# Retention and a squared-ReLU feed-forward on one core: first casts on VectorE, fillers from one zero tile, joined retention clusters from a later group

## The chip, the cores and the metric

The kernel runs on one core of a Trainium2 chip. Its time is the device time of the whole program in microseconds (us), the median of several executions. A profile is taken of one execution; its span runs from the first to the last instruction. Engines are named as in the profile: PE (TensorE; PEld is its weight loads), DVE (VectorE), ACT (ScalarE), POOL (GpSimd) and SP (SyncE, whose queue issues nearly all DMAs here).

## The reference

```python
scores = scale * np.matmul(q, k.transpose(0, 1, 3, 2))     # 8 batches, 8 heads, 576 positions, 64 per head
gamma = 1.0 - 2.0 ** (-5.0 - np.arange(H))
Dmat = np.where(rel >= 0, gamma[:, None, None] ** rel[None, :, :], 0.0)   # rel = i - j
x = np.matmul(scores * Dmat[None], v)                      # causal, decaying with distance
x = x.transpose(0, 2, 1, 3).reshape(4608, 512)
h = x @ w_in                                               # 512 -> 2048
out = (np.maximum(h, 0) ** 2) @ w_out                      # 2048 -> 512
```

All inputs and the output are float32.

## The kernel before

**Units and groups.** The 4608 rows are cut into 36 units of 128: four per batch ("full"), and for every two batches one more that holds the last 64 positions of both ("tail"). Groups are one unit, one unit, and then 17 times two units. A group g goes through retention, which gives its `xT`, and through the feed-forward.

**Retention of a group.** Keys and queries are needed transposed (`kqT`). Then PE makes the scores (`psc`) and the state sums (`psS`, keys times values), DVE masks the scores (`rT`) and carries the states on (`Rm`, `stmp`, `R`), PE makes the outputs (`psO`, from states and from masked scores), and DVE scales these into `xT`. All of these products are 64x64, on quarters of the array. In an unjoined group this is two clusters on PE: `fa` (scores and sums), and `fb` (outputs, with a drain of PE between its two halves). From group `JOIN` on (line 218), clusters are joined: `f1` holds the first outputs of g and the scores of g+1, `f2` the sums of g+1 and the other outputs of g, and there is no drain. `add_casts` gives the casts of groups behind `JOIN` a due time one group earlier.

**Feed-forward of a group.** `ph` = x times w_in (64 matmuls of 256 columns, line 730), ACT's ReLU into `rl`, a square into `gT`, then times w_out into `po`: plainly for the first three groups and the last (line 771), and by seven Strassen products of half size for the others (line 823; DVE makes the sums `gS`).

**The start.** SP issues the first loads in the order of `FIRST`: the first pair of units (k, q, v; `p0`), a quarter of w_in, another, the second pair (`p2`), the other two quarters of w_in, the four quarters of w_out. They share four staging buffers ("wst"), so that a load can wait for the casts of an earlier one. Each weight quarter is cast to float16 half by POOL and half by ACT (line 306). The first four units come in as pairs (`add_unit_pair`): each row of a load is two neighbouring positions. k, q and v are cast as they are (`kx`, `qx`, `vx`, lines 395 and 398; k and v on POOL, q on ACT), PE transposes `kx` and `qx` (line 411) and brings rows of `kx` and `vx` into order by products with the permutation `perm` (`psn`, line 432). From unit 8 on, the transposes are DMA transposes on SP (line 363).

**Fillers.** 40 matmuls of 128x512 into one PSUM tile (`warm`, line 234) have the lowest priority and take the PE time for which the planner has nothing else. They read `ident` as weights and the zero tile `junk`, which DVE sets after its other constants (line 211).

**The planner.** Every step is a task with an engine, a due key, a duration and dependencies (`Schedule`). It plays the program through once with these durations, takes on each engine the ready task with the lowest key, and emits the instructions in the order that results. So durations decide an order that the hardware then follows: each engine runs its queue in order[...]. The planned durations of loads (`dma_task`), transposes (line 364) and stores (lines 783 and 877) are such numbers.

Of the kernel before, what the change touches and what calls it, by code (L numbers as in the profile page):

```python
# [10 lines left out]
FP16 = mybir.dt.float16  # L11
# [90 lines left out]
def kernel(  # L102
# [54 lines left out]
    w_out16 = const.tile([P, NF, DM], FP16, name="w_out16")  # L157


    ident = const.tile([P, P], FP16, name="ident")  # L160
    make_identity(nc, ident)

# [44 lines left out]
           "tail": gam_f[:, :, 0:64].rearrange("p n (c i) -> p c n i", c=1).to_broadcast([P, 2, NP, 64])}  # L207
    dec128 = const.tile([P, NP], FP32, name="dec128")
    nc.scalar.activation(out=dec128, in_=lnrow_R, func=ACTF.Exp, scale=128.0)
    junk = const.tile([P, 512], FP16, name="junk")  # L210
    nc.vector.memset(junk, 0.0)


    L = 2 * NF
    WARM = 40
    EARLY = 20
    SQ_ACT = (0, 1, 2, 3, 4, 5, 6)
    JOIN = 9
    XBAR = 8
    PAIRED = 4  # L220
    FIRST = ["p0", "w0", "w1", "p2", "w2", "w3", "w4", "w5", "w6", "w7"]
# [9 lines left out]
    def warm():  # L231
        if not warm_ps:
            warm_ps.append(ps_ff.tile([P, 512], FP32, name="warm", tag="ff"))
        nc.tensor.matmul(warm_ps[0], lhsT=ident, rhs=junk, start=True, stop=True)
    fill = []
    for _ in range(WARM):
        fill.append(add("PE", 10 ** 6, 0.3, warm, deps=fill[-1:], acq=() if fill else ("ff",)))
    sched.free("ff", fill[-1:])


# [14 lines left out]
    def dma_task(key, dur, fn, **kw):  # L255
        t = add("SP", key, dur, fn, deps=list(last_load), **kw)
        last_load[:] = [t]
        return t
# [18 lines left out]
    def add_load_pair(u):  # L277
        b, c = units[u][1:]
        for n, (name, src) in enumerate((("k", k), ("q", q), ("v", v))):
            def fn(n=n, name=name, src=src):  # L280
                if name != "q":
                    tile_of["stage", u] = stage.tile([P, 2, H, 2 * D], FP32, name="pair", tag="wst")
                x = tile_of[name + "32", u] = tile_of["stage", u][:, n % 2]
                nc.sync.dma_start(out=x, in_=src[b, :, c * P:(c + 2) * P, :].rearrange("h (p e) d -> p h (e d)", e=2))  # L284
            loaded[name, u] = loaded[name, u + 1] = dma_task(0, 1.4 if loaded else 2.3, fn,
                                                             acq=("wst",) if name != "q" else ())

    def add_weight(i):
# [41 lines left out]
    def add_unit(u, base):  # L330

        kind, b, c = units[u]
        tail = [tail_dec] if kind == "tail" else []
        xbar = u >= XBAR

        def sorted_cast(op, out_, in_):
            op(out=out_.rearrange("p (n b a d) -> p n b a d", n=2, b=2, a=2),  # L337
               in_=in_.rearrange("p (n a b) d -> p n b a d", n=2, a=2))

        def fk():  # L340
            t = tile_of["kq", u] = cast.tile([P, 2, H * D], FP16, name="kq16", tag="kq16")
            sorted_cast(nc.gpsimd.tensor_copy, t[:, 0], tile_of["k32", u])

        def fq():
            sorted_cast(nc.gpsimd.tensor_copy, tile_of["kq", u][:, 1], tile_of["q32", u])

        def fv():
            t = tile_of["v16", u] = cast.tile([P, H, D], FP16, name="v16", tag="v16")
            nc.gpsimd.tensor_tensor(  # L349
                out=t, in0=tile_of["v32", u],  # L350
                in1=vdec[kind].rearrange("p (h o) -> p h o", o=1).to_broadcast([P, H, D]), op=ALU.mult)
        ck = add("POOL", base, 0.65, fk, deps=[loaded["k", u]], acq=("kq",))
        cq = add("POOL", base + 1, 0.62, fq, deps=[loaded["q", u], ck])
        cv = add("POOL", base + 2, 1.1, fv, deps=[loaded["v", u]] + tail, acq=("v16",))
        for what, t in (("k", ck), ("v", cv)):
            for w in gate.get((what, u), []):
                sched.need(w, t)
        T["casts", u] = [ck, cq, cv]
        sched.free("ld", [ck, cq, cv])
        if xbar:  # L360
            def fx2():
                t = tile_of["kqT", u] = work.tile([P, 2 * NP, P], FP16, name="kqT", tag="kqT", bufs=6)
                nc.sync.dma_start_transpose(out=t, in_=tile_of["kq", u].rearrange("p x n -> p (x n)"))  # L363
            T["kqT", u] = [add("SP", -1, 2.0, fx2, deps=[ck, cq], acq=("kqT",), after=4.0)]
            return
        T["kqT", u] = []
        for i, cst in enumerate((ck, cq)):
            def ft(i=i):
                tile_of["psT", u, i] = ps_ff.tile([P, NP, P], FP16, name="psT", tag="ff")
                for hp in range(NP):  # L370
                    nc.tensor.transpose(tile_of["psT", u, i][:, hp, :], tile_of["kq", u][:, i, hp * P:(hp + 1) * P],
                                        ident)

            def fe(i=i):
                if i == 0:
                    tile_of["kqT", u] = work.tile([P, 2 * NP, P], FP16, name="kqT", tag="kqT", bufs=6)
                (nc.vector.tensor_copy if i else nc.scalar.copy)(
                    out=tile_of["kqT", u][:, i * NP:(i + 1) * NP], in_=tile_of["psT", u, i])
            t = add("PE", base + L + i, 0.22, ft, deps=[cst], acq=("ff",))
            e = add("DVE" if i else "ACT", base + L + 2 + i, 0.42 if i else 0.59, fe, deps=[t] + T["kqT", u],  # L380
                    acq=() if i else ("kqT",))
            sched.free("ff", [e])
            T["kqT", u].append(e)


    def add_unit_pair(u, base):

        xs = {}
        for name, eng, op in (("k", "POOL", nc.gpsimd.tensor_copy), ("q", "ACT", nc.scalar.copy),
                              ("v", "POOL", nc.gpsimd.tensor_copy)):  # L390
            def fc(name=name, op=op):
                t = tile_of[name + "x", u] = cast.tile([P, 2, H * D], FP16, name=name + "x", tag="kq16")
                x = tile_of[name + "32", u].rearrange("p h (e d) -> p h e d", e=2)
                if name == "v":
                    op(out=t.rearrange("p e (h d) -> p e h d", d=D), in_=x.rearrange("p h e d -> p e h d"))
                    return
                for e in range(2):
                    op(out=t[:, e].rearrange("p (n b a d) -> p n b a d", n=2, b=2, a=2),
                       in_=x[:, :, e].rearrange("p (n a b) d -> p n b a d", n=2, a=2))
            xs[name] = add(eng, base + "kqv".index(name), dict(k=1.3, q=1.2, v=1.2)[name], fc, deps=[loaded[name, u]],  # L400
                           acq=("kq",))
        sched.free("wst", [xs["k"], xs["q"]])
        sched.free("wst", [xs["v"]])
# [312 lines left out]
    def add_ff(g):  # L716
# [44 lines left out]
        for s, u in enumerate(us):  # L761
            end = base2 + NF * (s + 1)
            f2 = T["ff2"][-1:] if s == 0 else f2[-1:]

            cuts = [(0, DM)] if u != groups[-1][-1] else [(0, HM), (HM, DM)]
            for ci, (lo, hi) in enumerate(cuts):
                for fi in range(NF):
                    def f(fi=fi, s=s, u=u, lo=lo, hi=hi):
                        if fi == 0:
                            tile_of["po", u, lo] = ps_ff.tile([P, hi - lo], FP32, name="po", tag="ff")  # L770
                        nc.tensor.matmul(tile_of["po", u, lo], lhsT=tile_of["g", g][:, fi, s * P:(s + 1) * P],  # L771
                                         rhs=w_out16[:, fi, lo:hi], start=(fi == 0), stop=(fi == NF - 1))
                    f2.append(add("PE", base2 + NF * s + fi / len(cuts) + 8 * ci, 0.0025 + 0.2135 / len(cuts), f,
                                  deps=[sq[fi // nf]] + wcast[4 + fi // 4] + f2[-1:],
                                  acq=("ff",) if fi == 0 else ()))

                def fo(u=u, lo=lo, hi=hi):
                    if lo == 0:
                        tile_of["o", u] = o_pool.tile([P, DM], FP32, name="o", tag="o")
                    nc.scalar.copy(out=tile_of["o", u][:, lo:hi], in_=tile_of["po", u, lo])  # L780
                oc = add("ACT", end + 1, 0.12 + 0.47 / len(cuts), fo, deps=[f2[-1]], acq=() if lo else ("o",))
                sched.free("ff", [oc])
                st = add(*(("ACT", end + 1.1, 0.05) if g == len(groups) - 1 else ("SP", -0.5, 0.6)),
                         lambda u=u, lo=lo, hi=hi: store(u, tile_of["o", u], lo, hi), deps=[oc], after=2.5)
            sched.free("o", [st])
        sched.free("g", [f2[-1]])
# [2 lines left out]
    def add_strassen(g, us, base, sq):  # L789
# [84 lines left out]
        sched.free("g", [p4])  # L874
        T["ff2"].append(p4)
        for u, ds in ((uA, [d11, c12]), (uB, [d22, d21])):
            st = add("SP", -0.5, 0.6, lambda u=u: store(u, o_tile(u)), deps=ds, after=2.5)
            sched.free("o", [st])

    for g in range(len(groups)):  # L880
# [44 lines left out]
```

## Time and profile before

| | |
|---|---|
| median of 6 executions | 300.6 us (298.77 to 304.06) |
| the profiled execution | 298.77 us, span 296.8 us |
| granted TensorE clock | 1.00 |
| PE busy | 285.9 us (96%), 4464 matmuls |
| DVE, ACT, POOL busy | 192.0, 189.5, 97.1 us |
| moved by DMA | 54.16 MB, 145503 packets, 130481 of them under 512 B |
| chain that ended last, by engine | PE 77%, DMA 13%, SP's queue 5% |

A busy share is an average over stages. The page's part 2 cuts the span into 40 slices of 7.4 us; a digit of 9 stands for a slice that is at least 90% busy, and PEclk is the granted clock. A DMA share is the mean over 16 engines. Matmul records overlap, since matmuls are pipelined: the time from one start to the next tells more than a record's length. Lines such as L730 are lines of the kernel before; in the changed kernel everything behind line 212 stands one line earlier.

### The profile page before, as it was taken

The numbers are of one execution on the slowest core, as the hardware profiler recorded it, in microseconds if no ns is written. First come the engines' busy times: TensorE is split into PE (matmuls) and PEld (weight loads), VectorE is DVE, ScalarE is ACT, GpSimd is POOL, SyncE is SP. The second block draws the span as 40 slices with busy tenths as digits, with TensorE's granted clock in tenths as the row PEclk, the third lists the DMA queues.
The fourth block names the chain that finished last, engine by engine and source line by source line (L and its number), as shares of the span: only waits on it lengthen the run. The fifth ranks groups of instructions, "written<-read, shape, count | busy, mean of one in ns | idle before, by whom it ended". The sixth has DMA issues, their size and how long they took to land.

```text
span 296.8 us, 10350 instructions
## 1 busy us (share of the span) xinstructions
PE 285.9 (96%) x4464; PEld 235.2 (79%) x4464; DVE 192.0 (65%) x409; ACT 189.5 (64%) x355; POOL 97.1 (33%) x130
## 2 busy tenths in 40 slices
PE   4997899999999999999999999999999999999995
PEld 1456667588888888888888888888888888888874
DVE  1287579678477877587876767668777766462410
ACT  4556554286767757575758575857585768558861
POOL 5454486444242432524244343517251100000000
PEclk9999999999999999999999999999999999999999
DMA  8999979899799998989999999999999420101012
GB/s 207 360 336 385 336 164 251 173 227 179 180 198 214 210 157 207 195 196 188 234 151 241 181 202 182 195 231 215 233 164 215 124 73 2 73 3 73 0 73 71
DMA packets 145503, 54.16 MB, mean 182 GB/s; under 512 B 130481, under 2 KB 136881, under 8 KB 145457
## 3 DMA queue, kind: packets, MB, share of 16 engines
q1 hardware_dynamic: 145008, 52.97, 86.2%
q8 instruction: 35, 0.57, 0.8%
q10 hardware_dynamic: 448, 0.52, 0.7%
q14 instruction: 12, 0.09, 0.1%
HBM read 36.70 MB, written 9.44 MB: 155 GB/s over the span
## 4 chain that ended last, share of the span: by engine, by line
PE 77%; DMA 13%; SPq 5%; issue 1%; POOL 1%; ACT 1%; POOLq 0%
PE ph L730 36%; PE po L823 27%; PE po L771 7%; DMA wi<-in_moe_w_in_dram 7%; DMA q<-in_q_dram 5%; PE psO L324 4%; SPq L270 2%; PE psc L324 1%; PE psS L324 1%; DMA kqT<-kq 1%; SPq L363 1%; SPq L284 1%; POOL w_in L306 1%; SPq L294 1%; POOL kq L337 1%
## 5 line engine op out<-in xcount | busy, mean ns | idle before, releaser
L730 PE MATMUL ph<-xT,w_in 128*128 128x256 f16 (+1 forms) x1216 | 139.5, 267 | 2.3 <-issue 2.1
L730 PEld LDWEIGHTS <-w_in 128*128 128x128 f16 x1216 | 112.6, 98 | 16.8 <-issue 2.5
L738 ACT ACTIVATE rl<-ph 128x512 f16<-128x512 f32 x144 | 84.7, 588 | 49.9 <-PE ph L730 46.5
L748 ACT ACTIVATE gT<-rl 128x512 f16<-128x512 f16 x112 | 70.5, 630 | 3.6
L801 DVE TENSOR_TENSOR gS<-gT 128x512 f16<-128x512 f16 x60 | 29.8, 497 | 41.1 <-ACT gT L748 40.4
L823 PEld LDWEIGHTS <-gS 128*128 128x128 f16 x480 | 45.8, 98 | 6.2 <-DVE gS L801 0.5
L823 PE MATMUL po<-wT,gS 128*128 128x256 f16 x360 | 49.0, 273 | 0.0
L349 POOL TENSOR_TENSOR v<-v,vdec_full 128x512 f16<-128x512 f32 x28 | 30.4, 1087 | 38.1 <-DMA v<-in_v_dram 29.2
L823 PEld LDWEIGHTS <-gT 128*128 128x128 f16 x360 | 35.0, 98 | 4.1
L337 POOL CAST kq<-k 128x512 f16<-128x512 f32 x32 | 22.3, 698 | 35.4 <-DMA k<-in_k_dram 34.5
L337 POOL CAST kq<-q 128x512 f16<-128x512 f32 x32 | 21.6, 674 | 34.8 <-DMA q<-in_q_dram 34.8
L823 PE MATMUL po<-w_out,gT 128*128 128x256 f16 x240 | 31.1, 273 | 0.0
L616 DVE TENSOR_TENSOR xT<-psO,gam_full 128x512 f16<-128x512 f32 x36 | 23.9, 685 | 7.6 <-PE psO L324 7.5
L555 DVE TENSOR_TENSOR rT<-psc,mask 128x512 f16<-128x512 f32 x36 | 24.1, 682 | 4.0 <-PE psc L324 4.0
L750 DVE TENSOR_TENSOR gT<-rl 128x512 f16<-128x512 f16 x32 | 17.7, 555 | 13.0 <-ACT rl L738 12.8
L771 PE MATMUL po<-w_out,gT 128*128 128x512 f16 (+1 forms) x112 | 23.2, 349 | 0.0
L846 DVE TENSOR_TENSOR o<-po,u 128x256 f32<-128x256 f32 x30 | 12.6, 420 | 8.5 <-ACT u L836 6.0
L836 ACT COPY u<-po 128x256 f32<-128x256 f32 x30 | 11.0, 366 | 10.2 <-PE po L823 10.1
L801 DVE TENSOR_TENSOR gS<-gT,gS 128x512 f16<-128x512 f16 x30 | 16.0, 533 | 1.0
L801 DVE TENSOR_TENSOR gS<-gS,gT 128x512 f16<-128x512 f16 x30 | 15.5, 517 | 1.0
L771 PEld LDWEIGHTS <-gT 128*128 128x128 f16 x112 | 10.4, 98 | 7.0
L584 DVE TENSOR_TENSOR R<-stmp,dec 128x256 f16<-128x256 f32 x28 | 15.1, 538 | 0.9
(75 smaller groups left out, 254.3 us busy)
## 6 DMA issues: line engine op xcount, KB each, us to landing
out_dram<-o SPq DMA_DIRECT2D x31, 256.0 KB, 3.0
k<-in_k_dram SPq DMA_DIRECT2D x28, 256.0 KB, 4.8
q<-in_q_dram SPq DMA_DIRECT2D x28, 256.0 KB, 5.0
v<-in_v_dram SPq DMA_DIRECT2D x28, 256.0 KB, 5.0
wi<-in_moe_w_in_dram SPq DMA_DIRECT2D x4, 1024.0 KB, 8.6
wo<-in_moe_w_out_dram SPq DMA_DIRECT2D x4, 1024.0 KB, 10.5
pair<-in_k_dram SPq DMA_DIRECT2D x2, 512.0 KB, 5.1
pair<-in_q_dram SPq DMA_DIRECT2D x2, 512.0 KB, 6.4
```

The lines of the kernel that those rows point to most:

```text
L324: nc.tensor.matmul(out_, lhsT=lhsT, rhs=rhs, start=start, stop=True, skip_group_check=True, tile_position=(64 * row, 64 * col))
L337: op(out=out_.rearrange("p (n b a d) -> p n b a d", n=2, b=2, a=2), in_=in_.rearrange("p (n a b) d -> p n b a d", n=2, a=2))
L349: nc.gpsimd.tensor_tensor(out=t, in0=tile_of["v32", u], in1=vdec[kind].rearrange("p (h o) -> p h o", o=1).to_broadcast([P, H, D]), op=ALU. ...
L555: nc.vector.tensor_tensor(out=r, in0=tile_of["psc", g][:, :, cols(s)].rearrange("p a (n i) -> p a n i", i=64), in1=mask.rearrange("p (o r ...
L616: nc.vector.tensor_tensor(out=tile_of["x", g][:, :, s * P:(s + 1) * P].rearrange("p n (c i) -> p c n i", c=2), in0=tile_of["psO", g][:, :, ...
L730: nc.tensor.matmul(tile_of["ph", g, fb][:, j, :], lhsT=w_in16[:, m, fi * P:(fi + 1) * P], rhs=tile_of["x", g][:, m, :], start=(m == 0), st ...
L738: nc.scalar.activation(out=t, in_=tile_of["ph", g, fb], func=ACTF.Relu)
L748: nc.scalar.activation(out=t, in_=rl, func=ACTF.Square)
L750: nc.vector.tensor_tensor(out=t, in0=rl, in1=rl, op=ALU.mult)
L771: nc.tensor.matmul(tile_of["po", u, lo], lhsT=tile_of["g", g][:, fi, s * P:(s + 1) * P], rhs=w_out16[:, fi, lo:hi], start=(fi == 0), stop= ...
L801: nc.vector.tensor_tensor(out=Sx(k, h), in0=in0(h), in1=in1(h), op=op)
L823: nc.tensor.matmul(tile_of["pb", g, bank], lhsT=left(i), rhs=right[:, i, :], start=(start and i == 0), stop=(i == HF - 1), skip_group_chec ...
```

## The change

Five edits in one:

- `junk` is set as DVE's first instruction, and the fillers take a slice of it as weights instead of `ident`. Their planned durations become 0.43 for the first eight and 0.216 for the others.
- The casts of the first pair (u = 0) go to DVE; those of the second pair stay with POOL, ACT, POOL.
- `JOIN` goes from 9 to 12, so that groups 9, 10 and 11 keep unjoined clusters, and casts get the earlier due time from group 13 on instead of 10.
- The planned durations of the paired loads, of the DMA transposes and of the stores change.
- The planned durations of the paired casts go by engine.

```diff
+    junk = const.tile([P, 512], FP16, name="junk")
+    nc.vector.memset(junk, 0.0)
     ident = const.tile([P, P], FP16, name="ident")
     make_identity(nc, ident)
...
     nc.scalar.activation(out=dec128, in_=lnrow_R, func=ACTF.Exp, scale=128.0)
-    junk = const.tile([P, 512], FP16, name="junk")
-    nc.vector.memset(junk, 0.0)
...
-    JOIN = 9
+    JOIN = 12
...
-        nc.tensor.matmul(warm_ps[0], lhsT=ident, rhs=junk, start=True, stop=True)
+        nc.tensor.matmul(warm_ps[0], lhsT=junk[:, 0:P], rhs=junk, start=True, stop=True)
     fill = []
-    for _ in range(WARM):
-        fill.append(add("PE", 10 ** 6, 0.3, warm, deps=fill[-1:], acq=() if fill else ("ff",)))
+    for i in range(WARM):
+        fill.append(add("PE", 10 ** 6, 0.43 if i < 8 else 0.216, warm, deps=fill[-1:], acq=() if fill else ("ff",)))
...
-            loaded[name, u] = loaded[name, u + 1] = dma_task(0, 1.4 if loaded else 2.3, fn,
+            loaded[name, u] = loaded[name, u + 1] = dma_task(0, 1.6 if loaded else 3.0, fn,
                                                              acq=("wst",) if name != "q" else ())
...
-            T["kqT", u] = [add("SP", -1, 2.0, fx2, deps=[ck, cq], acq=("kqT",), after=4.0)]
+            T["kqT", u] = [add("SP", -1, 2.7, fx2, deps=[ck, cq], acq=("kqT",), after=3.0)]
...
-        for name, eng, op in (("k", "POOL", nc.gpsimd.tensor_copy), ("q", "ACT", nc.scalar.copy),
-                              ("v", "POOL", nc.gpsimd.tensor_copy)):
+        pool, act, dve = (("POOL", nc.gpsimd.tensor_copy), ("ACT", nc.scalar.copy), ("DVE", nc.vector.tensor_copy))
+        for name, (eng, op) in (("k", pool if u else dve), ("q", act if u else dve), ("v", pool if u else dve)):
...
-            xs[name] = add(eng, base + "kqv".index(name), dict(k=1.3, q=1.2, v=1.2)[name], fc, deps=[loaded[name, u]],
+            xs[name] = add(eng, base + "kqv".index(name), dict(POOL=1.2, ACT=1.15, DVE=0.85)[eng], fc, deps=[loaded[name, u]],
...
-                st = add(*(("ACT", end + 1.1, 0.05) if g == len(groups) - 1 else ("SP", -0.5, 0.6)),
+                st = add(*(("ACT", end + 1.1, 0.05) if g == len(groups) - 1 else ("SP", -0.5, 0.7)),
...
-            st = add("SP", -0.5, 0.6, lambda u=u: store(u, o_tile(u)), deps=ds, after=2.5)
+            st = add("SP", -0.5, 0.7, lambda u=u: store(u, o_tile(u)), deps=ds, after=2.5)
```

## The prediction

> **What bounds the kernel now.** First the page's part 2, to see which stages there are.
>
> ```profile
> PE   4997899999999999999999999999999999999995
> ...
> PEclk9999999999999999999999999999999999999999
> DMA  8999979899799998989999999999999420101012
> ```
>
> PE is full from the sixth slice (37 us) to the end, and its clock is granted in full throughout. Only the first five slices are open, and in these the DMA row is full. The stretch view (length; busy time and instructions of PE, weight loads, DVE, ACT, POOL; clock; DMA share; GB/s) says it more sharply:
>
> ```profile
> 2.30:13.00 10.70, 8.65 (x44) 4.02 (x44) 1.01 (x18) 4.66 (x12) 4.46 (x11) 1.00 1.09 336
> 13.00:19.00 6.00, 5.86 (x104) 2.68 (x105) 4.56 (x8) 3.33 (x5) 2.76 (x4) 1.00 1.19 301
> 19.00:35.00 16.00, 13.73 (x343) 10.85 (x328) 12.06 (x23) 10.38 (x16) 7.87 (x9) 1.00 1.05 382
> 35.00:42.00 7.00, 6.76 (x57) 4.88 (x56) 3.73 (x7) 5.08 (x8) 4.53 (x6) 1.00 0.93 193
> 60.00:130.00 70.00, 69.52 (x1156) 60.37 (x1154) 49.69 (x101) 48.85 (x93) 26.93 (x34) 1.00 1.11 192
> 130.00:230.00 100.00, 99.91 (x1674) 86.75 (x1673) 75.66 (x151) 66.64 (x129) 37.71 (x48) 1.00 1.11 205
> ```
>
> A DMA share over 1 from 2.3 to 35 us means that the 11 MB of first loads stream without a hole: no cast that frees a staging buffer sooner makes a weight land sooner. After 42 us PE has no hole. So the end moves only by (a) how much useful PE work is done by about 37 us, (b) PE time per group afterwards.
>
> For (a) the timeline and, from 17 us, the chain of waits:
>
> ```profile
> 4.35 6.21 PE L234 MATMUL warm<-junk,ident 128*128 128x512 f16 x20 [4.35 <-DVE junk L211]
> 4.92 1.17 POOL L398 CAST kx<-pair 128x512 f16<-128x512 f32 x2 [1.28 <-DMA pair<-in_k_dram]
> 6.64 1.14 ACT L398 CAST qx<-pair 128x512 f16<-128x512 f32 x2 [1.96 <-DMA pair<-in_q_dram]
> 8.43 1.04 POOL L395 CAST vx<-pair 128x1024 f16<-128x1024 f32 x1 [2.34 <-DMA pair<-in_v_dram]
> 10.40 0.61 PE L411 MATMUL psT<-ident,kx 128*128 128x128 f16 x8
> ```
>
> ```profile
> 27.20 1.35 PE ph L730 x21
> 28.55 1.64 issue
> 30.19 1.89 PE ph L730 x31
> ...
> 36.38 0.24 issue
> ```
>
> The keys are cast by 6.1 us, but their transposes start at 10.40: PE is in order and works off 20 fillers that waited until 4.35 for the zeros. And at 28.4 PE stops for 1.8 us, start to start, in the middle of a tile, with no semaphore to wait for. Page part 3 has "q8 instruction: 35" packets with 0.57 MB, 16 KB each; PE's 8,930 program rows divided among 35 are 256. Counting PE's rows in the trace, row 193 runs at 17.2 us, 449 at 23.72, 705 at 30.19 (the end of that stop) and 961 at 36.62 (the end of the 0.24): steps of 6.5 us. The packets of that queue start at 21.34, 27.59 and 34.01, some 4 us behind the row that lets them be asked for. While the first loads hold the DMA engines, **PE gets 256 instructions per 6.5 us**. That paces the start.
>
> **The change, part by part.**
>
> *Zeros first.* The memset (272 ns) opens DVE's queue, which starts at 0.88, and the fillers read it as weights too: the first runs at about 1.2 instead of 4.35, 3.15 us sooner. Before, matmuls were 430 ns apart for the first 3.7 us and 216 ns after. Now 21 stand ahead of the transposes: 8 x 430 + 13 x 216 ns = 6.25, end 7.45; I take 7.6. (If the fast pitch comes 3 us later, some seven more run at 430 and the end is 9.1; before could meet the same.) The eight lnrow memsets come 0.27 later; DVE waits for iota_p until 2.81 anyway.
>
> *Casts on DVE.* The trace has no SBUF-to-SBUF f32 cast on DVE. Nearest rows: "DVE CAST Rm" 413 ns for 256 elements from PSUM, and DVE's f32 passes of 512 from PSUM at 682. The Trainium skill, "VectorE: DVE Perf Modes", errata table, gives an SBUF copy in a double-rate mode 58 + 512/2 cycles at 0.96 GHz, 0.33 us. Two casts are then 0.65 by the rule, 1.36 by the slow row; I take 0.85, two at about the CAST row, for 1.17 on POOL: keys at 5.8 instead of 6.1, queries at 7.5, values at 9.2 (8.43 plus about 0.75). None is awaited: transposes start at 7.6, and values are needed only near 10.7. Even the slow ends fit (6.3, 8.0, 9.6). This edit is worth nothing by itself; without fillers in front it would be 0.3. A rule speaks against it: "SBUF — State Buffer" says that such a DVE copy locks the port it shares with GpSimd, and the other blocks for that instruction. By that rule, POOL work beside it would lose up to 0.85. But POOL's row after the mask (3.7) is then empty until w_in at 11.15. I take 0.
>
> *What follows from both.* The compiled order shows, up to row 193 (the products with Rm of unit 0), 40 fillers instead of 36, 0.86 us. So row 193 comes 2.95 - 0.86, some 2.1 us sooner: the key transposes at 7.6; their permuting products and 4 fillers (2.17, as before); query transposes, 4 products, 7 fillers (2.48 + 0.43): scores at 12.7 instead of 15.05; scores, sums and 8 fillers put row 193 at **15.0** instead of 17.2. DVE's rT, Rm, stmp (0.67 + 0.41 + 0.42 behind scores) end at 14.8, just ahead. POOL's R of unit 0 now stands before the w1 cast and moves that from 13.9 to about 15.4; w1 is multiplied only after 21. On SP the second pair can be issued once these casts end, 9.1 instead of 9.5, behind loads still streaming: 0.
>
> *Through the load stage.* Row 193 at 15.0 gives 449 at 21.5, 705 at 28.0, 961 at 34.4 by the same step. Does the data keep up? 16 ph matmuls of unit 0 now stand before the second pair's transposes; w2 is cast by 23.0 and w3 by 27.2, both before row 705 needs them. From 28.0: 49 ph at 55 ns (2.7), psO (1.1), 8 po at 216 ns (1.7), 7 ph at 109 ns (0.8) come to 34.3; the second w_out block (cast by 33.0) fits. Both orders hold the same work before row 961, so PE enters the full stage at 34.4 instead of 36.6: **-2.2 us**. It stays if inputs follow: the store that blocks SP until 42.21 (it waits for unit 0's output) goes out at about 40.7, taking 1.5 us from DMA's hole at 41 to 43. Unit 7's values were cast at 56.85 with scores at 58.04: room 1.2, plus 1.5.
>
> *JOIN 9 to 12.* For (b) I measured each cluster from the last wide matmul before it to the first after, less one pitch (109 ns). Unjoined: 0.74 (scores and sums at 113.98) + 1.02 to 1.11 (outputs), with the hole of the drain in it:
>
> ```profile
> 120.97 0.19 PE L324 MATMUL psO<-kqT,R 64*64 64x64 f16 x1
> 121.26 0.32 PE L324 MATMUL psO<-rT,v 64*64 64x64 f16 x16
> ```
>
> Joined: 0.60 + 0.86 = 1.46 (159.10 and 164.96). The difference is 0.3 per group, three groups: **+0.9**. In return the transition comes later. At 144.29 a joined cluster cost 0.84, not 0.60: the transposed keys of unit 21 were issued at 140.93 and took 3.8 us. At 137.07 another had 0.24 too much. Lead grew in the unjoined stage: unit 9's transpose was issued 5.6 us before its scores, unit 17's 12.2. Three more such groups give some 4 us more, so these waits can go: between 0 and -0.5, I take **-0.4**.
>
> *The planner's numbers* (loads, transposes, stores) issue nothing; they move stores and loads around transposes on SP, and POOL's keys. In the order, a transpose now follows one load more, 1.3 us of 256 KB at 200 GB/s; its scores also stand later in PE's order (group 5: by 22 matmuls, 2.4 us). Between -0.2 and +1; I take 0.
>
> Sum: -2.2 + 0.9 - 0.4 = **-1.7 us**, from the profiled execution's own 298.77 (span 296.8 plus 2.0 around it) to 297.1. That execution was the fastest of six; against their median, 300.6, this is **298.9**.
>
> **Rivals.**
> 1. *The start gives nothing* (weights decide, not the fetch). For: DMA share over 1; w3 lands at 26.05 whatever is done. Against: with w3 cast at 27.2 PE still stops at 28.4 for 1.8 us. Then +0.9 and no more: 301.5, within 0.5%.
> 2. *Inputs come late*: reordered SP and a PE 2.2 us ahead turn into waits for transposed keys at group 5 or the later transition. For: the wait at 144, DMA share 1.11. Against: the lead above. It eats 1 to 2 us: 300.4.
> 3. *The clock falls*, the slower side. All 40 fillers are gone by 15.0 (before: four after psO, to 18.9), and PE is to stop from about 25.7 to 28.0. The skill, "TensorE: Matmul & The Clock Gate", holds that PE idle for a window of some 3.4 us drops to half clock. The row: 1.8 us cost no clock. By the row my 2.3 us is free; by the rule it decides from 3.4 us on, if the fetch takes a microsecond longer. Then half speed for one window, 3.4 us at 1.7 each, and again at the next stop: +3.4 - 1.7 + 0.9 for lost lead, 303.2.
>
> **How the numbers follow.** Forecast 0.53, rival 1 0.16, rival 2 0.16, rival 3 0.15. About 0.5% (1.5 us) is what a measurement can tell from no change; the forecast lies just beyond it (-0.57%), so it gives 0.34 faster and 0.19 same; rival 2 gives 0.05 faster, 0.08 same, 0.03 slower; rival 1 0.13 same, 0.03 slower; rival 3 0.15 slower. Faster 0.39, same 0.40, slower 0.21. The forecast's own range is 297.6 to 300.2; with the rivals, 297.0 to 302.8.
>
> **What would show it.** First filler at 1.2, key transposes near 7.6, scores of unit 0 near 12.7; PE's stop without semaphore ending near 28 instead of 30.19; group 3's first ph at 57.4 instead of 59.56; groups 9 to 11 with two clusters of 0.74 + 1.05. Wrong if that stop still ends at 30, if PEclk falls below 9, or if PE waits for kqT over 0.5 us in total.

## The result, and the profile after

The changed kernel takes 299.63 us (median of 35 executions, 298.02 to 300.55) against 300.94 for the kernel before, measured beside it (72 executions, 298.77 to 305.18). The ratio is 0.9954, with a 95% interval of 0.9942 to 0.9967: 1.4 us less. A second measurement of the same pair (e5, below) gave 0.9957 (0.9937 to 0.9978). The ratios leave out the few executions that are over 1.5% above the fastest of their kernel; they are not quotients of the medians given here.

The profiled execution of the changed kernel took 299.23 us (span 297.4), which is more than the 298.77 of the profile before. There is no contradiction: that profile of before was of the fastest of its 72 executions. A second profile of before, e4 below, has a span of 298.6, and readings of "before" are taken from both from here on.

The page's part 2 for the changed kernel (busy tenths in 40 slices, granted clock, DMA share) stands as before, but the first slice is open no longer:

```profile
PE   8989999999999999999999999999999999999995
...
PEclk9999999999999999999999999999999999999999
DMA  7999999999998979997979699989999981202012
```

The timeline of its first 10 us (start, length, engine, line, operation, tiles, count, and in brackets the idle time before and what ended it) shows the edits of the start at work:

```profile
0.93 0.27 DVE L161 MEMSET junk<- 128x256 uint32 x1 [0.93 <-PEq L908]
...
1.25 7.54 PE L233 MATMUL warm<-junk 128*128 128x512 f16 x21 [1.25 <-DVE junk L161]
...
4.92 0.76 DVE L397 CAST kx<-pair 128x512 f16<-128x512 f32 x2 [1.02 <-DMA pair<-in_k_dram]
...
6.71 0.76 DVE L397 CAST qx<-pair 128x512 f16<-128x512 f32 x2 [1.03 <-DMA pair<-in_q_dram]
...
8.50 0.69 DVE L394 CAST vx<-pair 128x1024 f16<-128x1024 f32 x1 [1.03 <-DMA pair<-in_v_dram]
8.63 0.61 PE L410 MATMUL psT<-ident,kx 128*128 128x128 f16 x8
```

The first filler runs at 1.25, the first pair's casts are on DVE and take 0.76 and 0.69, and the key transposes start at 8.63 instead of 10.40 (in a second profile of the changed kernel, e5, at 7.31: there 7 fillers ran at the slow pitch, here 13).

One reading carries most of what follows. The first `ph` matmul of group 3 and that of group 18 are two marks that every order of instructions passes with the same PE work behind it (before the first, in every order: 192 `ph`, 64 `po`, 128 scores, 128 sums, 176 outputs and all 40 fillers). So the time to mark 3 is "the start", and the time from mark 3 to mark 18 is "the rest". Both are read from the records of single matmuls:

| kernel | what it has of the change | ratio to before (95%) | mark 3, us | mark 3 to 18, us |
|---|---|---|---|---|
| before, and e4 | nothing | 1 | 59.56, 59.62 | 215.7, 217.5 |
| e6_zeros | zero tile first | 0.9986 (0.9960 to 1.0011) | 59.89 | 216.9 |
| e7_casts | casts on DVE | 0.9978 (0.9955 to 1.0000) | 60.06 | 219.0 |
| e1_start | both, with the fillers' durations | 0.9956 (0.9936 to 0.9976) | 58.72 | 216.3 |
| e2_join | JOIN 12 | 1.0016 (0.9999 to 1.0033) | 59.59 | 217.3 |
| e3_sp | SP's planned durations | 1.0160 (1.0118 to 1.0203) | 61.58 | 219.4 |
| e8_after_join9 | all but JOIN | 1.0032 (1.0007 to 1.0057) | 58.29 | 221.5 |
| e9, e10 | all but SP's durations | 0.9897 (0.9848 to 0.9947), 0.9926 (0.9903 to 0.9949) | 58.77, 58.84 | 216.8, 217.0 |
| e11_loads | the same, and the loads' durations | 0.9932 (0.9912 to 0.9951) | 57.31 | 216.9 |
| e12_transposes | the same, and the transposes' duration | 0.9964 (0.9945 to 0.9983) | 58.48 | 218.2 |
| changed kernel, and e5 | all | 0.9954 (0.9942 to 0.9967), 0.9957 (0.9937 to 0.9978) | 57.32, 57.73 | 218.5, 217.9 |

Against the means of before (59.6 and 216.6) the change wins 2.1 us in the start and loses 1.6 in the rest. The marks are of single profiles, in which the rest alone scatters by 1.8 us for one kernel; the ratios are of many executions. The start repeats better: e1, e9 and e10, whose orders differ only through JOIN, have mark 3 at 58.7 to 58.8. And the 1.6 us are too many: -2.1 + 1.6 is not the measured -1.4, mainly because the first profile of before is 2.2 us below its median. Against e4 alone, whose time is the median, the rest loses 0.7, and the sum fits.

### The profile page after: what moved, and what is told of

Same layout as the page of the kernel before. It is cut to its first block, busy times and chain, and to the rows that moved or that the text cites. A ratio compares the mean times of both kernels' runs of the same rounds, so it can differ in the third digit from the quotient of the medians.

```text
span 297.4 us, 10349 instructions
## 1 busy us (share of the span) xinstructions
PE 288.3 (97%) x4464; PEld 235.3 (79%) x4464; DVE 193.3 (65%) x414; ACT 188.5 (63%) x353; POOL 95.9 (32%) x127
## 4 chain that ended last, share of the span: by engine, by line
PE 71%; DVE 12%; ACT 10%; DMA 3%; issue 2%; POOL 1%; ACTq 0%; DVEq 0%; POOLq 0%
PE ph L729 29%; PE po L822 26%; PE po L770 6%; ACT rl L737 5%; DVE gS L800 4%; ACT gT L747 4%; PE psO L323 4%; PE warm L233 3%; DMA wi<-in_moe_w_in_dram 3%; DVE gT L749 2%; PE psc L323 1%; DVE xT L615 1%; DVE rT L554 1%; PE psS L323 1%; DVE stmp L579 1%
## 5 line engine op out<-in xcount | busy, mean ns | idle before, releaser
L800 DVE TENSOR_TENSOR gS<-gT 128x512 f16<-128x512 f16 x60 | 28.3, 473 | 41.1 <-ACT gT L747 40.5
L336 POOL CAST kq<-q 128x512 f16<-128x512 f32 x32 | 22.2, 693 | 28.7 <-DMA q<-in_q_dram 28.7
L615 DVE TENSOR_TENSOR xT<-psO,gam_full 128x512 f16<-128x512 f32 x36 | 23.7, 685 | 10.4 <-PE psO L323 10.4
L749 DVE TENSOR_TENSOR gT<-rl 128x512 f16<-128x512 f16 x32 | 19.7, 619 | 12.1 <-ACT rl L737 12.0
L554 DVE TENSOR_TENSOR rT<-psc,mask 128x512 f16<-128x512 f32 x36 | 24.1, 682 | 1.9 <-PE psc L323 1.9
L800 DVE TENSOR_TENSOR gS<-gS,gT 128x512 f16<-128x512 f16 x30 | 16.5, 551 | 1.0
L822 PE MATMUL po<-wT,gT 128*128 128x256 f16 x120 | 15.8, 273 | 0.2 <-DVE o L845 0.2
```

The lines of the kernel that those rows point to most:

```text
L554: nc.vector.tensor_tensor(out=r, in0=tile_of["psc", g][:, :, cols(s)].rearrange("p a (n i) -> p a n i", i=64), in1=mask.rearrange("p (o r ...
L615: nc.vector.tensor_tensor(out=tile_of["x", g][:, :, s * P:(s + 1) * P].rearrange("p n (c i) -> p c n i", c=2), in0=tile_of["psO", g][:, :, ...
L749: nc.vector.tensor_tensor(out=t, in0=rl, in1=rl, op=ALU.mult)
L800: nc.vector.tensor_tensor(out=Sx(k, h), in0=in0(h), in1=in1(h), op=op)
L822: nc.tensor.matmul(tile_of["pb", g, bank], lhsT=left(i), rhs=right[:, i, :], start=(start and i == 0), stop=(i == HF - 1), skip_group_chec ...
```

## The experiments

**The kernel before, again (e4).** No edit.

> The kernel before, unchanged, for a second profile: the first was of the fastest execution. If rows 193 to 961 of PE stand again at 17.2, 23.7, 30.2 and 36.6 us with the stop that ends at 30.2, the pace of 6.5 us is a property of the program and not of that one execution. If they scatter by more than 1 us, single profiles can't settle a difference of 1.4 us. Time 300 to 301 us.

It took 300.61 us. Rows 193, 449, 705 and 961 came at 18.0, 24.1, 28.9 and 35.3, against 17.2, 23.7, 30.2 and 36.6 in the first profile: steps of 6.1, 4.8 and 6.4, and no fixed pace. PE's timeline of e4 where the first profile stops for 1.8 us:

```profile
25.91 2.82 PE L730 MATMUL ph<-xT,w_in 128*128 128x128 f16 x45
28.90 1.28 PE L730 MATMUL ph<-xT,w_in 128*128 128x128 f16 x20 [0.17 <-issue]
```

0.17 us of "issue" is left of the stop, 0.39 us from start to start. Group 2 therefore starts 1.3 us sooner than in the first profile (34.50 against 35.78), and still mark 3 is the same, 59.62. What took it back stands in e4's timeline of DVE, and in the outputs that PE then waits for:

```profile
46.99 1.57 DVE L750 TENSOR_TENSOR gT<-rl 128x512 f16<-128x512 f16 x2
...
49.42 2.01 DVE L750 TENSOR_TENSOR gT<-rl 128x512 f16<-128x512 f16 x2
51.35 0.68 DVE L555 TENSOR_TENSOR rT<-psc,mask 128x512 f16<-128x512 f32 x1
...
54.24 0.42 DVE L580 TENSOR_TENSOR stmp<-psS,Rm 128x256 f32<-128x256 f32 x1
```

```profile
54.72 0.22 PE L324 MATMUL psO<-kqT,Rm 64*64 64x64 f16 x2 [0.75 <-DVE stmp L580]
```

DVE works without a hole from 43 to 55 us (the sums `wT` of the w_out quarters, squares), and the scores that PE began at 48.52 are masked only at 51.35. The two profiles have the same order, so they can be compared matmul by matmul: of PE's lead of 1.3 us, 0.5 go at two small waits at 47.3 (for ACT's `rl`) and 49.0 (for DVE's `kqT`), and 0.8 at this one. So from 43 us on the limit of this kernel is mainly DVE's queue, and PE's own stop at 28 cost nothing.

**The parts of the start.** First the two edits together (e1), with JOIN and SP's numbers as before. The planned durations of the fillers and of the paired casts are the changed kernel's here too (not in this diff):

```diff
+    junk = const.tile([P, 512], FP16, name="junk")
+    nc.vector.memset(junk, 0.0)
     ident = const.tile([P, P], FP16, name="ident")
...
-        nc.tensor.matmul(warm_ps[0], lhsT=ident, rhs=junk, start=True, stop=True)
+        nc.tensor.matmul(warm_ps[0], lhsT=junk[:, 0:P], rhs=junk, start=True, stop=True)
...
+        pool, act, dve = (("POOL", nc.gpsimd.tensor_copy), ("ACT", nc.scalar.copy), ("DVE", nc.vector.tensor_copy))
+        for name, (eng, op) in (("k", pool if u else dve), ("q", act if u else dve), ("v", pool if u else dve)):
...
```

> Only the two edits of the start: zero tile first (and read as weights), first pair's casts on VectorE with their planned durations; JOIN stays 9 and SP's planned durations stay old. My theory (the start is paced, what it gains is kept): first filler 1.2, row 961 of PE 2 to 3 us sooner than before, and the end as well: -2.0 to -3.0 us (ratio 0.990 to 0.993). Rival 'given back': the gain is eaten by new waits behind 40 us even without the other edits: -0.5 to +0.5 us. Rival 'start gives nothing': row 961 at 36.6 as before, 0.

The ratio, 0.9956, is 1.3 us: the sign of the theory, not its size, and as much as the whole change gives. Row 961 came at 35.3, as in e4, and mark 3 at 58.72. So against e4 the 0.9 us are won behind row 961: from 36 us to mark 3 PE's waits come to 0.4 us here and to 1.0 in e4. Why PE waits less there in this order stays open.

Then the zero tile alone (e6; the first two hunks of that diff, with the fillers' planned durations as before), which leaves every engine's order as it was but for the zero tile itself, and the casts alone (e7; the last hunk, with the casts' planned durations):

> Only the zero tile first, read as weights by the fillers too; the order of every engine's other instructions is that of before. First filler 1.25 instead of 4.36. If PE's start is the limit: key transposes at about 8.2, row 193 near 15 (before 17.2 to 18.2), first ph of group 2 near 32.5 (before 34.5 to 35.8) and the end 1 to 2 us sooner (ratio 0.993 to 0.997). If the weights, whose last quarter of w_in is cast at 27.2 whatever is done, are the limit: the same first ph of group 2 and 0.

> Only the first pair's casts on VectorE and the planned durations of the paired casts. Prediction: nothing by itself behind fillers that end at 9.5 to 10.4 anyway; the planner puts four fillers fewer first, so up to 0.9 us of the start. If the casts are the gain of the change: -1 us or less (ratio under 0.997). If the new order of the second pair's transposes costs: above 0.

Both ratios, 0.9986 and 0.9978 (0.4 and 0.7 us), have intervals that reach 1. The fillers' planned durations are in e1 and in neither of these; how much of e1's gain is theirs was not tried. In e6 the first part happened in full: scores of unit 0 at 11.79 instead of 15.05. PE's timeline then shows where it went:

```profile
15.61 0.30 PE L324 MATMUL psS<-v,kn 64*64 64x64 f16 x16
16.60 0.40 PE L411 MATMUL psT<-ident,kx 128*128 128x128 f16 x4 [0.69 <-POOL kx L398]
17.16 0.40 PE L411 MATMUL psT<-ident,kx 128*128 128x128 f16 x4 [0.16 <-POOL kx L398]
19.45 0.92 PE L411 MATMUL psT<-ident,qx 128*128 128x128 f16 x8 [1.89 <-ACT qx L398]
```

PE waits 2.7 us for the second pair, and the casts it waits for are waiting for the loads (timeline of e6, all engines):

```profile
15.93 1.17 POOL L398 CAST kx<-pair 128x512 f16<-128x512 f32 x2 [0.19 <-DMA pair<-in_k_dram]
...
18.77 1.14 ACT L398 CAST qx<-pair 128x512 f16<-128x512 f32 x2 [3.63 <-DMA pair<-in_q_dram]
...
20.58 1.04 POOL L395 CAST vx<-pair 128x1024 f16<-128x1024 f32 x1 [3.48 <-DMA pair<-in_v_dram]
```

So the second pair's landing, not PE's start, is what the first 22 us wait for once PE starts early. All profiles say the same: the values of that pair are cast from between 19.3 and 21.0 us on, and PE begins its products with them 1.4 to 2.0 us after the end of that cast where the zero tile comes late (before, e2, e3, e4, e7), but 0.05 to 0.5 us after it where the tile comes first. An earlier start pays only if the order has other work to put ahead of it. The changed kernel's order has. Its PE timeline, first profile and then e5:

```profile
17.75 1.07 PE L729 MATMUL ph<-xT,w_in 128*128 128x128 f16 x16
...
20.72 0.62 PE L410 MATMUL psT<-ident,qx 128*128 128x128 f16 x8
21.77 1.02 PE L431 MATMUL psn<-vx,perm 128*128 128x512 f16 x4 [0.43 <-POOL vx L394]
22.63 2.26 PE L729 MATMUL ph<-xT,w_in 128*128 128x128 f16 x32
```

```profile
16.42 1.07 PE L729 MATMUL ph<-xT,w_in 128*128 128x128 f16 x16
...
20.04 0.61 PE L410 MATMUL psT<-ident,qx 128*128 128x128 f16 x8 [0.58 <-ACT kqT L418]
21.78 1.02 PE L431 MATMUL psn<-vx,perm 128*128 128x512 f16 x4 [1.14 <-POOL vx L394]
22.64 2.27 PE L729 MATMUL ph<-xT,w_in 128*128 128x128 f16 x32
```

At 16.4 to 17.8 the two executions are 1.3 us apart, at 21.8 they are level, because both then wait for the second pair's values. But 16 `ph` matmuls lie behind them, which in the kernel before come after that point.

**JOIN alone (e2).**

```diff
-    JOIN = 9
+    JOIN = 12
```

> Only JOIN 9 to 12. My prediction's terms: three groups at +0.3 and the transition's waits gone, +0.9 - 0.4 = +0.5 us (ratio 1.0017). Rival 'the drain is the whole price, no lead is won': +0.9 and more (1.003). Rival 'the lead is worth more than the drain': below 0.

1.0016 is +0.5 us, the prediction's figure; the interval (0 to +1.0 us) leaves the first rival just possible and the third all but out.

**SP's planned durations alone (e3).**

```diff
-            loaded[name, u] = loaded[name, u + 1] = dma_task(0, 1.4 if loaded else 2.3, fn,
+            loaded[name, u] = loaded[name, u + 1] = dma_task(0, 1.6 if loaded else 3.0, fn,
...
-            T["kqT", u] = [add("SP", -1, 2.0, fx2, deps=[ck, cq], acq=("kqT",), after=4.0)]
+            T["kqT", u] = [add("SP", -1, 2.7, fx2, deps=[ck, cq], acq=("kqT",), after=3.0)]
...
-                st = add(*(("ACT", end + 1.1, 0.05) if g == len(groups) - 1 else ("SP", -0.5, 0.6)),
+                st = add(*(("ACT", end + 1.1, 0.05) if g == len(groups) - 1 else ("SP", -0.5, 0.7)),
...
-            st = add("SP", -0.5, 0.6, lambda u=u: store(u, o_tile(u)), deps=ds, after=2.5)
+            st = add("SP", -0.5, 0.7, lambda u=u: store(u, o_tile(u)), deps=ds, after=2.5)
```

> Only the planned durations of loads, DMA transposes and stores. Prediction: 0 (between -0.2 and +1 us). Rival: these numbers bring the gain, since they give loads and transposes a better order: -1 us or less. Rival: they bring the small new waits of PE behind 50 us: +1 us or more.

+4.8 us (six executions; the interval is 3.5 to 6.1), far outside the prediction's -0.2 to +1. Planned durations that issue nothing put 22 fillers instead of 20 ahead of the transposes (they now start at 12.06, against 10.40 and 11.21), and mark 3 moves by 2 us. Behind the transition at group 9, a `ph` waits 2.0 us for `xT`.

**The changed kernel with JOIN back at 9 (e8), and without SP's durations (e9).**

```diff
-    JOIN = 12
+    JOIN = 9
```

> The changed kernel with JOIN back at 9. By the prediction's terms (JOIN 12 costs 0.5) it is 0.5 us faster than the changed kernel: ratio to before 0.994. Rival, after what the planned durations of SP did alone (+4.8 us, of it 2 us of waits at the transition at group 9): with JOIN 9 these come back, +1 to +3 us against the changed kernel, ratio 1.000 to 1.006; then JOIN 12 is what makes the new planned durations bearable.

> The changed kernel without the planned durations of SP (they stay those of before). If these cost in this order too: faster than the changed kernel by 1 us or more, ratio to before near 0.992. If the parts add (start -1.3, JOIN +0.5): -0.8 us, 0.9973. If they help in this order: slower than the changed kernel, ratio 0.998 or more.

The parts do not add. With SP's new numbers, JOIN 9 costs 2.3 us against the changed kernel (1.0032 against 0.9954), where JOIN 12 alone cost 0.5. The view of PE's waits (engine, tile, line, releaser, sum in us, times, longest), from 60 us on, says by what, in e8:

```profile
PE po L822 <- DVE gS L800: 3.4, 5, 1.4
PE ph L729 <- DVE xT L615: 1.3, 1, 1.3
PE po L822 <- ACT u L835: 0.5, 1, 0.5
```

and without SP's numbers (e9) the kernel comes out faster than the changed one: 0.9897, but from only six executions, and the two intervals still meet. It is measured again as e10.

**The changed kernel (e5), that kernel again (e10), and each number by itself (e11, e12)**, all on one chip. e11 and e12 add to e10 the first or the second hunk of e3's diff.

> The changed kernel again, for a second profile and beside the next three. Ratio 0.995. If its first profile's start (first ph of group 2 at 32.4) was luck, it comes at 33.5 here as with JOIN back at 9; if the waits of PE for gS and stmp behind 60 us belong to its order, they are here again, 2 us or more in sum.

> The changed kernel without SP's planned durations, a second time, on the same chip as the changed kernel. If these durations cost in this order: 1 us or more faster than the changed kernel here too (ratio to before 0.991 to 0.993). If the first result was the scatter of six executions: the same as the changed kernel, 0.995.

> That kernel with only the planned durations of the paired loads changed (1.6 and 3.0). If the loads' numbers are what costs, because they put four more fillers ahead of the first transposes and shift the second pair: key transposes 0.9 later than without them, and as slow as the changed kernel, 0.995. If they cost nothing: 0.992.

> The same with only the planned duration of the DMA transposes changed (2.7, then 3.0). If it is this number that costs, by an order in which PE's products stand too close behind DVE's and SP's work from group 5 on: the start as without it, but 1 us or more of waits behind 60 us, 0.995. If it costs nothing: 0.992. If both this and the loads' run come out at 0.992, it is only their combination (or the stores' number).

Medians: 299.11 (e5), 298.75 (e10), 298.63 (e11), 299.42 (e12), before 300.31. The loads' numbers cost nothing; they bring mark 3 from 58.8 to 57.3. In the whole time nothing of this 1.5 us shows: e11's 0.9932 is e10's 0.9926 within the intervals. The profile of e11 is of an execution 1.1 us below its median, so its rest (216.9) is likely shorter than that of most; what takes the 1.5 us back is open. What PE met in the start of e10, in its timeline, is a run of 40 `ph` that needs the third quarter of w_in before that is cast:

```profile
22.00 1.50 PE L730 MATMUL ph<-xT,w_in 128*128 128x128 f16 x24
24.69 1.07 PE L730 MATMUL ph<-xT,w_in 128*128 128x128 f16 x16 [1.19 <-POOL w_in L306]
```

With 21 fillers and the loads' numbers (e11 and the changed kernel) PE runs 32 `ph`, then the scores, and of this wait 0.1 us is left. In e11:

```profile
22.48 2.25 PE L730 MATMUL ph<-xT,w_in 128*128 128x128 f16 x32
24.66 0.44 PE L324 MATMUL psc<-kqT 64*64 64x64 f16 x32
```

The transposes' number likely costs about 1 us (0.9964; its interval meets that of e10 only in its last 0.0004; by the medians it is 0.7). PE's waits from 60 us on, in e11, e12 and e5:

```profile
PE po L823 <- DVE gS L801: 0.3, 1, 0.3
```

```profile
PE po L823 <- DVE gS L801: 1.6, 4, 0.9
```

```profile
PE po L822 <- DVE gS L800: 1.0, 3, 0.6
```

e9 and e10 have 0.5 and 0.3 us. The first profile of the changed kernel has 0.7 for `gS` and 0.8 for three other tiles of DVE; e8, which holds that number too, had 3.4. So in the changed start's order it is probably the order of PE against DVE that this number worsens; in the order of before it does not (0.7 in e3 with it, 0.8 in e6 without). The stores' number was not tried alone.

e10 and e11 come out 0.3 and 0.2% below the changed kernel, on the same chip, but their intervals overlap its own: a version that surely beats it is not shown. e11 has the earliest mark 3 (57.31), but not the shortest rest.

## Why the prediction was right, and where its reasons were not

The forecast was 298.9 with a sum of -1.7 us; the result is -1.4, between forecast and second rival.

- **The start, -2.2.** Right in size in the profiles: mark 3 was to come at 57.4 and came at 57.32 and 57.73. None of the three signs of being wrong came: in neither profile of the changed kernel does PE stop at row 705, the clock row is 9, and no wait for DMA-transposed keys is listed. Rows 193 to 961 were to come at 15.0, 21.5, 28.0 and 34.4; they came at 15.4, 22.0, 27.2 and 33.7, in e5 at 14.1, 22.0, 27.1 and 33.9.
- **Its reason, "that paces the start": PE's 256 instructions per 6.5 us.** This step failed. PE does stop at rows 449, 705 and 961 in other profiles too, but for anything from nothing to 1.9 us, so no pace follows; and the stop does not set the start: in e4 it is 1.5 us shorter at row 705 and mark 3 is the same. In its place the runs show two limits in series: the second pair's landing (its values are cast from 19.3 to 21.0 us on, whatever PE does before), then, shown in e4, DVE's queue from 43 us on.
- **"Zeros first" as the whole gain.** First filler and casts came as worked out (1.25 for 1.2; casts 0.76 and 0.69 for 0.85 and 0.75). Alone each gave nothing at mark 3: 59.89 and 60.06. Together, with the fillers' planned durations, they gave 0.9 there, and against e4 none of it by row 961; the loads' planned numbers, which I put at 0, gave another 1.5 (e11 against e9 and e10). With these numbers row 961 comes at 33.5 to 33.9 instead of 35.0 to 35.3 (e1, e9, e10): 16 `ph` ahead of the second pair's values are in all these orders, so what the numbers add is an order without the long wait for w_in. That the whole time is shorter by it is not shown.
- **Fillers until 7.6.** 8.63 and 7.31: the number of fillers at the slow pitch, which I took as 8, is 6 to 14 in the profiles. At 21.8 us it makes no difference.
- **DVE casts, rule and row.** The Trainium skill, "VectorE: DVE Perf Modes", errata table, gave 0.33 for a cast; here two take 0.76 together, 0.42 for the record of each and 0.34 from start to start, and the slow bound was 0.68. Whether such a cast blocks GpSimd's port no run here shows, since POOL stood idle beside it.
- **JOIN, +0.9 - 0.4.** Right alone (+0.5). In the changed kernel groups 9 to 11 cost 0.74 + 1.02 where joined ones cost 0.60 + 0.86, as worked out (one output cluster of its first profile has 0.4 more, a wait for `stmp`), and PE's waits for `kqT` are gone: the waits from 60 us on list none in any profile with JOIN 12. With JOIN 9 they vary between executions: the same view lists none in the first profile of before, 1.2 us in e4, and in e7:

```profile
PE psc L324 <- DMA kqT<-kq: 2.3, 2, 1.4
```

- **The planner's numbers, 0.** This term was mis-sized. Alone they cost 4.8 us; in the changed kernel the profiles have over a microsecond less in the start (57.5 against 58.8 without them) and 1.3 more in the rest (218.2 against 216.9), and the ratios put the sum at up to +0.9 (0.9957 against 0.9926, intervals that overlap); my bound was -0.2 to +1. The rivals' waits for keys did not come; waits for `gS` did.
- **Rivals.** The first had the right kind of cause (loads, though the second pair and, in e1 and e10, the third quarter of w_in, not w3) and holds for the zero tile alone. The third did not come: the clock row is 9 throughout.

That the sum came out close is in part luck. The start's gain has another source than I gave it, the planner's numbers moved both parts where I had 0, and the two edits of the start alone (e1) already give the -1.3 of the whole -1.4. What the rest lost cannot be told from these profiles: 1.6 us against the mean of both profiles of before, 0.7 against e4, where the sum had 0.5.

## What to carry to other kernels

A stop that one profile shows is not yet a limit: take a second profile of the unchanged kernel, and fix a mark that all orders pass with the same work behind them, before a pace is built on it. Starting an engine sooner pays only as far as the order gives it work up to the next landing; look up that landing before the saved time is counted. Where a planner turns durations into an order, every duration is an edit of every queue: try it alone and in its place, since its worth (+4.8 us alone, under 1 us in the whole) and even its neighbours' (JOIN +0.5 alone, -2.3 in the whole) depend on the rest.

## What the hardware showed besides

- The pitch of the first fillers (430 ns, later 216) changed after 6 fillers in e6, 8 in the first profile of before, 12 in e4, 7 in e5, 13 in the first profile of the changed kernel and 14 in e3: between 2.5 and 5.9 us after PE's first matmul, different between executions of one program.
- The instruction packets of PE (16 KB each) start 6.1 to 7.1 us apart while the first loads hold the DMA engines (21.34, 27.59, 34.01 in the first profile of before; 20.35, 26.42, 32.66 in e4). The stop without a releaser at row 705 ended 1.3 to 1.5 us after the end of such a packet wherever it was seen: at 30.19 for 28.72 in the first profile of before, 30.25 for 28.77 in e7, 31.70 for 30.40 in e3, 28.90 for 27.46 in e4. How long PE stands there is how much sooner it comes to that row: at 28.33, 29.24, 29.78 and 28.51. In e6, where PE waited for data, two packets are 9.5 us apart, so they are no clock of their own; what sets their time was not tested.
